# A bucketed-attention and MLP kernel: the hash beside the FFN in two passes, with its row groups added by VectorE and its transfers behind the homes

## The chip, the cores and the metric

One core of one Trainium2 chip. The metric is the device time of one execution in microseconds, the median over several runs. A profile is one further execution, taken with the hardware profiler. Engines carry the profile's names: PE (TensorE, with PEld for its weight loads), DVE (VectorE), ACT (ScalarE), POOL (GpSimd) and SP (SyncE, which issues nearly all transfers).

## The reference

Attention in which a query sees only keys of its own bucket, followed by a two-layer MLP over all tokens. A bucket is six bits: the signs of the products with six random directions.

```python
# q, k, v: (4, 8, 768, 64); proj: (64, 6); w_in: (512, 2048); w_out: (2048, 512)
q_bits = (np.einsum('bhsd,dk->bhsk', q, proj) > 0)
k_bits = (np.einsum('bhsd,dk->bhsk', k, proj) > 0)
mask = q_bucket[:, :, :, None] == k_bucket[:, :, None, :]   # buckets: the bits as numbers
scores = scale * np.matmul(q, k.transpose(0, 1, 3, 2))
scores = np.where(mask, scores, -1000000000.0)
attn = softmax(scores)
x = (attn @ v).transpose(0, 2, 1, 3).reshape(B * S, H * D)
h = x @ w_in
g = h * np.clip(h + 3.0, 0.0, 6.0) / 6.0
out = g @ w_out
```

## The kernel before

**Numbers in two parts.** PE multiplies in fp32r, which keeps fewer bits than fp32. Every operand is therefore split into a high part (`hi`, the rounded number) and a low part (`lo`, what the rounding left), and a product is the sum of three passes: hi with hi, hi with lo, lo with hi.

**Attention.** There are 32 heads (4 batches of 8) of 768 rows, in 192 steps of 128 queries, 6 steps (t = 0 to 5) to a head. `raw` holds a head's transposed queries (partitions 0 to 63) and keys (64 to 127). `split_qk` (L282) makes four tiles of it: `q1` (high part of both), `k2` (low part of the keys, then their high part), `q2` (high part of the queries, then their low part) and `k1` (high part of the keys). Half of these rows are copied across partitions by transfers. `scores` (L374) multiplies queries and keys; the mask comes out of the same product, because 12 more rows of `q1` and `k1` hold the bits of both as large numbers of either sign. Then `lowest` (L391, row minimum, DVE), `exponential` (L402, ACT), `flip` (L426, DVE transposes blocks of 32 and the tile goes to a scratch `fd` in HBM), `move` (L434, four transfers bring it back, transposed, into one of two homes, `spare` and `px`), `split_p` (L451, `ph` by ACT, `pl` by DVE for half c = 0 and by POOL for half c = 1), `values_whole` (L505, PE: `acc` from `vv` with `ph` and `pl`, the half c = 1 first) and `output` (L529, `y` by ACT, then to `xs` in HBM; the other half of each `y` is added to `xs` by a transfer that POOL issues, L522).

**The hash.** `hash_qk` (L325) makes `z`, 108 rows by 768 columns in two halves: three passes for each half, `pjl` (low part of the directions) with `q1` (L334), then `pjh` (their high part, in two placings) with `k2` (L335) and with `q2` (L336). The 44 rows from 64 on hold the bits' products, each direction with both signs. `bits` (L340) compares them with a limit per row and multiplies by a value per row (L352, DVE), writes the result into the spare rows of `q1`, and copies 12 of these rows into `k1` by a transfer.

**The MLP.** `gemm1` (L653, `h`), `gate` (L679: ACT `g`, DVE `h`, ACT `gb`, DVE `gb`) and `gemm2` (L695, `po`). `ffn` (L927) works through chunks of 256 tokens, 16 blocks of 128 of the hidden width each.

**Order.** PE, DVE, ACT and POOL run in the order in which the code is written, each engine in order; SP runs its transfers in order too. From step 101 on (`paced`) attention steps and FFN blocks alternate: `beside_ffn` (L1115) writes one of each, and the FFN's parts A to D come between the parts of the step. In one step PE takes the products with `vv` (every other step), `gemm1`, the hash if there is one, `gemm2`, then the scores. The hash of head n stands in the step whose look-ahead has t = 4 in the head before; the scores that need its bits come two steps later. There are 14 such hashes (heads 18 to 31). In the step after a hash the row minimum is written behind DVE's `gb` (`behind`, L1136), in others ahead of it.

**Transfers at the end of a step.** `moves` is a list of deferred transfers: the copies of `q1`'s rows, the keys' rows of the next head (`get_k_rows`, L246) and half of an output store. One of them is issued in each step, ahead of the four home transfers of `move`.

Of the kernel before, what the change touches and what calls it, by code (L numbers as in the profile page):

```python
# [10 lines left out]
F32 = mybir.dt.float32  # L11
F32R = mybir.dt.float32r
# [31 lines left out]
def lsh_attention_moe(  # L44
# [10 lines left out]
    nc = tc.nc  # L55
    B, H, D, S = qkT.shape
# [3 lines left out]
    HW = S // 2  # L60
# [8 lines left out]
    cp = ctx.enter_context(tc.tile_pool(name="cp", bufs=1))  # L69
    sp = ctx.enter_context(tc.tile_pool(name="sp", bufs=2))  # L70
# [5 lines left out]
    def dma(out: bass.AP, in_: bass.AP):  # L76
        nonlocal last
        last = nc.sync.dma_start(out=out, in_=in_)  # L78

    paced = False  # L80
# [12 lines left out]
    def bank(shape, name: str, tag: str | None = None):  # L93

        nonlocal turn
        if tag is None:
            tag = ("pt", "pu")[turn % 2]
            turn += 1
        return ps.tile(shape, F32, name=name, tag=tag, bufs=2)
# [4 lines left out]
    def pair(name: str):  # L104

        nonlocal pair_turn
        pair_turn += 1
        tag = "s" if ffn_on or pair_turn % 2 else "po"
        return ps.tile([P, 2, 512], F32, name=name, tag=tag, bufs=1)
# [7 lines left out]


    pjl = cp.tile([P, ZM], F32R, name="pjl")
    pjh = cp.tile([P, ZM + ZK - D], F32R, name="pjh")  # L120
    nc.vector.memset(pjl[:].bitcast(F32), 0.0)
    nc.vector.memset(pjh[:].bitcast(F32), 0.0)
    pjk, pjq = pjh[:, :ZM], pjh[:, ZK - D :]


    nc.vector.memset(thr[:], 0.0)
    nc.vector.memset(val[:], 0.0)
    for r, one, big in ((D, 0, -BIG), (ZK, 1, 1.0)):
# [3 lines left out]
        nc.vector.memset(val[r : r + 2 * NB], big * (1, -1)[1 - one])  # L132
        nc.vector.memset(val[r : r + NB], big * (1, -1)[one])
    nc.vector.memset(three[:], 3.0)

    raw0 = sp.tile([P, S], F32, name="raw0", tag="raw", bufs=1)[:]
    dma(out=raw0, in_=qkT[0, 0])
    pr = sp.tile([P, NB], F32, name="pr", tag="pr", bufs=1)
# [88 lines left out]
    NJ = B * H  # L227
# [4 lines left out]
    GT = GF + FT  # L232
    raws, vrs, state, zs = {}, {}, {}, {}
# [11 lines left out]

    def get_k_rows(i: int):  # L246
        b, h = divmod(i, H)
        moves.append(lambda: dma(out=raws[i][D:], in_=qkT[b, h, D:]))

    def get_v(i: int):  # L250
        b, h = divmod(i, H)
# [3 lines left out]
    def hash_weights():  # L255
        for x in range(2):
            c = ZK + (1 - x) * NB
            nc.vector.tensor_scalar_mul(pjh[:, c : c + NB], pr[:], (1.0, -1.0)[x])
        for r, c in ((slice(0, D), D), (slice(D, P), ZK)):
            pos = pjh[r, ZK + NB : ZM]  # L260
            nc.vector.tensor_sub(pjl[r, c + NB : c + 2 * NB], pr[r], pos.bitcast(F32))
            nc.vector.tensor_sub(pjl[r, c : c + NB], pos.bitcast(F32), pr[r])

    def spans(i: int):

# [11 lines left out]

    copied = None
    subs = []
    moves = []  # L280

    def split_qk(i: int, copy):  # L282
        nonlocal copied
# [41 lines left out]
    def hash_qk(i: int):  # L325
        k1, k2, q1, q2 = state[i]
        if paced:
            z = zs[i] = [bank([P, HW], f"z{i}_{j}") for j in range(2)]
        else:
            both = pair(f"z{i}")  # L330
            z = zs[i] = [both[:, j, :HW] for j in range(2)]
        for j in range(2):
            c = slice(j * HW, (j + 1) * HW)
            nc.tensor.matmul(z[j][:ZM], lhsT=pjl[:], rhs=q1[:, c], start=True, stop=False)  # L334
            nc.tensor.matmul(z[j][:ZM], lhsT=pjk, rhs=k2[:, c], start=False, stop=False)  # L335
            nc.tensor.matmul(z[j][:ZM], lhsT=pjq, rhs=q2[:, c], start=False, stop=True)  # L336
        if not paced:
            zs[i] = both

    def bits(i: int):  # L340
        k1, k2, q1, q2 = state[i]
        z = zs.pop(i)

        if isinstance(z, list):
            whole = [(slice(j * HW, (j + 1) * HW), z[j][D:ZM], False) for j in range(2)]
        elif i == 0:
            whole = [(slice(j * HW, (j + 1) * HW), z[D:ZM, j, :HW], False) for j in range(2)]
        else:
            whole = [(slice(0, S), z[D:ZM, :, :HW], True)]
        for c, of, both in whole:  # L350
            to = q1[D:ZM, c]
            nc.vector.tensor_scalar(  # L352
                out=to.rearrange("p (j c) -> p j c", j=2) if both else to, in0=of,
                scalar1=thr[D:ZM], scalar2=val[D:ZM], op0=ALU.is_gt, op1=ALU.mult,
            )
            if i == 0:
                nc.scalar.copy(k1[D : D + 2 * NB, c], q1[ZK:ZM, c].bitcast(F32))  # L357
            elif c.stop == S:
                dma(out=k1[D : D + 2 * NB].bitcast(F32), in_=q1[ZK:ZM].bitcast(F32))
# [678 lines left out]
    def lead(j: int):  # L1038

        i, t = divmod(j, KT)  # L1040
        n = i + 1
        alone = j <= GF + LA
        if t == 0 and n < NJ:
            split_qk(n, nc.scalar.copy if ffn_on else nc.gpsimd.tensor_copy)
        if t in (1, 4) and not paced:
            add()
        if t == (4 if paced else 2):
            if i:
                split_v(i)
        if t == (3 if paced else 2):  # L1050

            if n + 1 < NJ and n != H + 1:
                get_qk(n + 1)
                if paced:
                    get_k_rows(n + 1)
        if t == (5 if paced else 3) and n < NJ:
            get_v(n)
        hashed = t == 3 and n < NJ and alone and j != GB - 1
        if hashed:
            hash_qk(n)  # L1060
        scores(j)
        if hashed:
            bits(n)
        if t == (5 if paced else 4) and n + 1 < NJ:
            scale_q(n + 1)
# [33 lines left out]
    with tc.manual_schedule(engines={ET.PE, ET.DVE, ET.Activation, ET.Pool}):  # L1099
# [15 lines left out]
        def beside_ffn(k: int):  # L1115
# [42 lines left out]
            paced = True  # L1158
# [25 lines left out]
                moves.pop(0)()  # L1184
            if GT <= k + 1 < NS:
                move(k + 1)

            place_in_chunk = (k - GT) % NFC
            if subs and (k % 2 and (k < GT or place_in_chunk != NFC - 1) or k > GT and place_in_chunk == 0):
# [5 lines left out]
        for k in range(NS + LT + 2):  # L1195
# [4 lines left out]
            i, t = divmod(k, KT)  # L1200
# [5 lines left out]
                load_first_x()  # L1206
            if k == HK:
                late["x"] = sp.tile([P, S], F32, name="late", tag="raw", bufs=1)
            for c in range(2):
                transp(k, c)  # L1210
            if k + 1 < end:
# [8 lines left out]
            whole = False  # L1220
            for _ in range(1 if k != HK else 2):
                if vnext < k - k % 2:
                    whole = value_half()
# [3 lines left out]
            if whole and k >= GF:  # L1227
                output(vnext // 2 - 1)
                whole = False
# [98 lines left out]
```

## Time and profile before

| | us |
|---|---|
| Median of 3 runs (lowest and highest) | 976.4 (975.54, 976.92) |
| The profiled execution | 973.11 |
| Its span, first to last instruction | 971.3 |
| PE busy in the span | 948.0 (98%), 6306 matmuls |
| DVE busy | 723.5 (74%) |
| ACT busy | 625.0 (64%) |
| POOL busy | 473.6 (49%) |

A row of the timeline reads: start, length, engine, line of the kernel, operation, output<-inputs, shape, count, and in brackets the idle time of the engine before it with what ended it. A row of a group reads: line, engine, operation, output<-inputs, shapes, count, then busy time in all, mean ns of one, idle time before them and its releasers. Matmuls are pipelined: one shows as 0.34 us and the next begins before it ends, so the cost of one is read from the starts.

### The profile page before, as it was taken

What the parts mean: (1) busy time and instruction counts of PE and PEld (TensorE: products, weight loads), DVE (VectorE), ACT (ScalarE), POOL (GpSimd) and SP (SyncE); (2) the same over time, 40 slices, a digit from 0 to 9 for tenths busy, and PEclk for the clock granted to TensorE, in tenths of its full rate; (3) what the DMA queues carried; (4) which work ended last, traced back from release to release, by engine and by line L of the source; (5) the groups of instructions that cost most, each with busy time, mean ns of one, the idle gap of its engine ahead of it and who ended that gap; (6) DMA issues with size and microseconds to landing.
All of it is one profiled execution on the core that took longest, in us unless ns stands there. A gap on an engine that the chain in (4) does not pass through costs nothing.

```text
span 971.3 us, 19460 instructions
## 1 busy us (share of the span) xinstructions
PE 948.0 (98%) x6306; PEld 873.6 (90%) x6306; DVE 723.5 (74%) x1470; ACT 625.0 (64%) x1421; POOL 473.6 (49%) x582
## 2 busy tenths in 40 slices
PE   8999999999999999899999999999999999999997
PEld 7999888999989999799899899989899899889896
DVE  7999988888569999877878878878777874342422
ACT  6898875655478988667766666666666664333332
POOL 6777744665537776455555545555545432000000
PEclk9999999999999999999999999999999999999999
DMA  3567579100035554787898788788887772101000
GB/s 117 140 156 188 131 224 377 58 1 1 6 119 119 115 142 112 192 252 233 238 267 234 231 256 241 230 267 236 243 258 233 211 227 71 44 1 44 1 22 22
DMA packets 113613, 152.06 MB, mean 157 GB/s; under 512 B 13876, under 2 KB 82612, under 8 KB 113512
## 3 DMA queue, kind: packets, MB, share of 16 engines
q1 hardware_dynamic: 108472, 144.79, 48.8%
q0 software_dynamic: 5040, 6.03, 5.3%
q8 instruction: 50, 0.82, 0.4%
q14 instruction: 51, 0.42, 0.2%
HBM read 77.34 MB, written 54.00 MB: 135 GB/s over the span
## 4 chain that ended last, share of the span: by engine, by line
PE 79%; DVE 8%; DMA 4%; ACT 4%; issue 3%; POOL 1%; SPq 1%; ACTq 0%; DVEq 0%; POOLq 0%
PE h L661 25%; PE acc L500 6%; PE po L704 6%; PE po L699 6%; PE po L700 6%; PE acc L513 6%; PE pt L418 5%; PE s L389 5%; PE s L387 5%; DMA spare<-fd 2%; DVE p L396 2%; DVE pl L479 2%; ACT ph L475 1%; SPq L78 1%; DVE qq L352 1%
## 5 line engine op out<-in xcount | busy, mean ns | idle before, releaser
L408 ACT ACTIVATE p<-p,m 128x768 f32<-128x768 f32 x192 | 180.2, 939 | 113.4 <-DVE p L396 105.2
L396 DVE TENSOR_SCALAR_CACHE_REDUCE p<-s 128x768 f32<-128x768 f32 x192 | 182.7, 952 | 24.9 <-PE pt L418 12.4
L684 DVE SCALAR_TENSOR_TENSOR h<-g,h 128x256 f32<-128x256 f32 x192 | 81.1, 423 | 102.0 <-ACT g L683 99.0
L683 ACT ACTIVATE g<-h,three 128x256 f32<-128x256 f32 x192 | 91.2, 475 | 94.9 <-PE h L661 94.0
L661 PE MATMUL h<-xh,w 128*128 128x256 f32 x1024 | 146.8, 282 | 0.0
L661 PEld LDWEIGHTS h<-xh,w 128*128 128x128 f32 x1024 | 134.9, 188 | 4.2 <-ACT xh L650 0.6
L429 DVE STREAM_TRANSPOSE p<-p 128x768 f32<-128x768 f32 x90 | 88.1, 979 | 65.2 <-ACT p L408 65.1
L477 POOL TENSOR_TENSOR pl<-spare,ph 128x384 fp32r<-128x384 f32 x45 | 45.8, 1018 | 127.3 <-ACT ph L475 71.4
L479 DVE TENSOR_TENSOR pl<-pt,ph 128x384 fp32r<-128x384 f32 x196 | 100.0, 550 | 4.0 <-ACT ph L475 3.5
L387 PE MATMUL s<-kk,qq 76*128 76x384 f32 x384 | 100.5, 343 | 2.0 <-ACT kk L357 1.5
L389 PE MATMUL s<-kk,qq 128*128 128x384 f32 x384 | 100.4, 343 | 0.0
L700 PE MATMUL po<-w,gb 128*128 128x512 f32 x250 | 98.4, 393 | 0.0
L699 PE MATMUL po<-w,gb 128*128 128x512 f32 x250 | 98.3, 393 | 0.0
L475 ACT CAST ph<-pt 128x384 fp32r<-128x384 f32 x196 | 86.1, 474 | 14.3 <-PE pt L418 13.0
L216 POOL TENSOR_TENSOR w<-wr,w 128x128 fp32r<-128x128 f32 x128 | 71.9, 593 | 45.2 <-ACT w L210 41.9
L418 PE MATMUL pt<-ident,p 128*128 128x128 f32 x612 | 86.2, 275 | 1.9 <-DVE pl L479 1.1
L689 ACT CAST gb<-h 128x256 fp32r<-128x256 f32 x141 | 52.4, 372 | 54.5 <-DVE h L684 26.8
L661 PE MATMUL h<-xl,w 128*128 128x256 f32 x512 | 81.2, 280 | 0.0
L418 PEld LDWEIGHTS pt<-ident,p 128*128 128x128 f32 x612 | 72.5, 141 | 8.9 <-PE pt L418 1.5
L704 PE MATMUL po<-w,gb 128*128 128x512 f32 x250 | 78.6, 395 | 1.5 <-DVE gb L690 1.5
L318 POOL TENSOR_TENSOR kk<-raw,qq 64x192 fp32r<-64x192 f32 (+1 forms) x73 | 65.4, 920 | 25.1 <-ACT qq L304 21.7
L387 PEld LDWEIGHTS s<-kk,qq 76*128 76x128 f32 x384 | 66.6, 190 | 11.7 <-ACT kk L357 2.0
(153 smaller groups left out, 2150.9 us busy)
## 6 DMA issues: line engine op xcount, KB each, us to landing
fd<-p SPq DMA_DIRECT2D x90, 384.0 KB
spare<-fd SPq DMA_DIRECT2D x180, 96.0 KB
px<-fd SPq DMA_DIRECT2D x180, 96.0 KB
kk<-qq SPq DMA_DIRECT2D x62, 192.0 KB
wr<-in_w_in SPq DMA_DIRECT2D x16, 512.0 KB
wr<-in_w_out SPq DMA_DIRECT2D x16, 512.0 KB
raw<-in_qkT SPq DMA_DIRECT2D x19, 384.0 KB
vr<-in_v SPq DMA_DIRECT2D x32, 192.0 KB
```

Of the source, the lines that this page charges most:

```text
L387: nc.tensor.matmul(s[:, c, :HW], lhsT=q1[:KM, us], rhs=half(k1[:KM], c), start=True, stop=False)
L389: nc.tensor.matmul(s[:, c, :HW], lhsT=q2[:, us], rhs=half(k2, c), start=False, stop=True)
L396: nc.vector.tensor_scalar(out=pr_[:], in0=s[:, :, :HW], scalar1=CAP, scalar2=None, op0=ALU.min, op1=ALU.min, accum_out=m[:],)
L408: nc.scalar.activation(pr_[:], pr_[:], AF.Exp, bias=m[:], scale=-1.0, accum_out=sms[b][:, t, h : h + 1])
L418: nc.tensor.transpose(pt[:, x], probs[g][0][:, c, x * P : (x + 1) * P], ident[:])
L475: nc.scalar.copy(hi, pt)
L479: lows.append(lambda: engine.tensor_sub(lo, pt, hi.bitcast(F32)))
L661: nc.tensor.matmul(hp, lhsT=wi[:, wp, wc], rhs=x[cc][xp], start=(k == 0 and cc == 0), stop=(k == 2 and cc == NCC - 1),)
L683: nc.scalar.activation(r[:], hp, AF.Relu, bias=three[:], scale=1.0)
L699: nc.tensor.matmul(po[u], lhsT=gh[:, us], rhs=wo[:, 0], start=(fc == 0), stop=False)
L700: nc.tensor.matmul(po[u], lhsT=gh[:, us], rhs=wo[:, 1], start=False, stop=False)
L704: nc.tensor.matmul(po[u], lhsT=gl[:, us], rhs=wo[:, 0], start=False, stop=(fc == NFC - 1))
```

## The change

In the FFN stage alone (`paced`) the hash takes another form:

- **Weights.** `pjs` has 132 columns: the low part of the directions in columns 12 to 23, the high part in 108 to 119. Read from column 0 it places the keys' products, read from column 12 the queries' products, 12 rows lower. `short_weights` builds it once on POOL at step 100, in the place of `pjh`.
- **Passes.** `q2` and `k2` each hold both parts of their numbers, one in each half of the partitions, and `pr` has the directions in both halves. So one pass of `q2` and one of `k2` give both products, with the low part of the directions in rows 0 to 23 of `z` and with the high part in rows 96 to 119. `q1` is not read. A half takes two passes in place of three, each into a single bank as before.
- **Sum and threshold.** ACT copies rows 0 to 23 of each half to rows 96 to 119 of the next head's `raw` (free at that time), DVE adds rows 96 to 119 of `z` to them, and one threshold over 768 columns reads the sum from SBUF and writes 24 rows of `q1`. Before, two thresholds of 384 columns read `z` from PSUM.
- **Limits.** The limits and values per row are in a new tile, `limits`, filled by eight POOL memsets at the start.
- **Transfers.** The bits' copy to `k1` and the keys' rows of the next head go to a new list, `behind_home`, which is issued whole behind the home transfers of the step. The keys' rows are asked for at t = 4 and no longer at t = 3.

```diff
+    def short_weights():
+
+        pjs = cp.tile([P, ZK + NR + NQ], F32R, name="pjs", tag="pjh")
+        nc.gpsimd.memset(pjs[:].bitcast(F32), 0.0)
+        short.extend([pjs[:, : ZK + NR], pjs[:, NQ:]])
...
     def hash_qk(i: int):
         k1, k2, q1, q2 = state[i]
         if paced:
-            z = zs[i] = [bank([P, HW], f"z{i}_{j}") for j in range(2)]
...
+            for j in range(2):
+                c = slice(j * HW, (j + 1) * HW)
+                z = bank([P, HW], f"z{i}_{j}")
+                zs[i].append(z)
+                nc.tensor.matmul(z[: ZK + NR], lhsT=short[1], rhs=q2[:, c], start=True, stop=False)
+                nc.tensor.matmul(z[: ZK + NR], lhsT=short[0], rhs=k2[:, c], start=False, stop=True)
+            return
...
         if isinstance(z, list):
-            whole = [(slice(j * HW, (j + 1) * HW), z[j][D:ZM], False) for j in range(2)]
...
+            r = slice(ZK, ZK + NR)
+            both = raws[i + 1][r] if i + 1 < NJ else sp.tile([P, S], F32, name=f"raw{i + 1}", tag="raw", bufs=1)[r]
+            for j in range(2):
+                nc.scalar.copy(both[:, j * HW : (j + 1) * HW], z[j][:NR])
+            for j in range(2):
+                c = slice(j * HW, (j + 1) * HW)
+                nc.vector.tensor_add(both[:, c], z[j][r], both[:, c])
+            nc.vector.tensor_scalar(
+                out=q1[D : D + NR], in0=both, scalar1=ths[r], scalar2=vas[r], op0=ALU.is_gt, op1=ALU.mult,
+            )
+            behind_home.append(lambda: dma(out=k1[D : D + NQ].bitcast(F32), in_=q1[D + NQ : D + NR].bitcast(F32)))
+            return
...
                 get_qk(n + 1)
-                if paced:
-                    get_k_rows(n + 1)
+        if t == 4 and paced and n + 1 < NJ and n != H + 1:
+            get_k_rows(n + 1)
...
             if GT <= k + 1 < NS:
                 move(k + 1)
+            while behind_home:
+                behind_home.pop(0)()
...
+            if k == GT - 2:
+                short_weights()
```

How the rows stand at one hash, that of head 27 (at 653.73 us in the profile of before). Numbers behind a tile's name are buffer numbers. First PE, from the last products of `gemm1` to the first of `gemm2`, before:

```order
L661 MATMUL h_0_7_9034<-xl_0_8573,w_2678 128x256 x4
L334 MATMUL z_0_9047<-qq_8825,pjl 108x384
L335 MATMUL z_0_9047<-kk_8824,pjh 108x384
L336 MATMUL z_0_9047<-qq_8825,pjh 108x384
L334 MATMUL z_1_9048<-qq_8825,pjl 108x384
L335 MATMUL z_1_9048<-kk_8824,pjh 108x384
L336 MATMUL z_1_9048<-qq_8825,pjh 108x384
L699 MATMUL po_0_8615<-w_2644,gb_0_6_9023 128x512
```

And PE at the same place now:

```order
L698 MATMUL h_0_7_9057<-xl_0_8596,w_2687 128x256 x4
L354 MATMUL z_0_9070<-qq_8849,pjs 120x384
L355 MATMUL z_0_9070<-kk_8848,pjs 120x384
L354 MATMUL z_1_9073<-qq_8849,pjs 120x384
L355 MATMUL z_1_9073<-kk_8848,pjs 120x384
L736 MATMUL po_0_8638<-w_2653,gb_0_6_9046 128x512
```

Two of six passes are gone and nothing else moves on PE. Next DVE from the flip to the row minimum of that step, before:

```order
L429 STREAM_TRANSPOSE p_9021<-p_9021 128x768
L684 SCALAR_TENSOR_TENSOR h_0_7_9034<-g_0_7_9061,h_0_7_9034 128x256
L479 TENSOR_TENSOR pl_0_9065<-spare,ph_0_9064 128x3x128
L352 TENSOR_SCALAR qq_8825<-z_0_9047,thr,val 44x384
L352 TENSOR_SCALAR qq_8825<-z_1_9048,thr,val 44x384
L690 TENSOR_TENSOR gb_0_7_9084<-h_0_7_9034,gb_0_7_9084 128x256
L396 TENSOR_SCALAR p_9088,m_9087<-s_9074 128x768
```

And DVE now, in the same stretch of the step:

```order
L466 STREAM_TRANSPOSE p_9044<-p_9044 128x768
L721 SCALAR_TENSOR_TENSOR h_0_7_9057<-g_0_7_9082,h_0_7_9057 128x256
L516 TENSOR_TENSOR pl_0_9086<-spare,ph_0_9085 128x3x128
L377 TENSOR_TENSOR raw_9019<-z_0_9070,raw_9019 24x384
L377 TENSOR_TENSOR raw_9019<-z_1_9073,raw_9019 24x384
L378 TENSOR_SCALAR qq_8849<-raw_9019,limits 24x768
L727 TENSOR_TENSOR gb_0_7_9109<-h_0_7_9057,gb_0_7_9109 128x256
L433 TENSOR_SCALAR p_9113,m_9112<-s_9097 128x768
```

Three instructions stand where two stood, ahead of `gb` and the row minimum. ACT's two copies (L374) stand behind the `ph` cast of half c = 0 and ahead of the gate's `gb` cast. Last SP from the keys' and queries' rows of the next head (`raw`) to the values (`vr`), before:

```order
L78 DMA raw_8995<-in_qkT 64x768 x2
L78 DMA xs_128<-y_0_8867 64x512
L78 DMA fd_8965<-p_8958 128x768
L78 DMA px<-fd_8911 32x4x192 x4
L78 DMA fd_9028<-p_9021 128x768
L78 DMA spare<-fd_8965 32x4x192 x3
L78 DMA kk_8824<-qq_8825 12x768
L78 DMA spare<-fd_8965 32x4x192
L78 DMA vr_9123<-in_v 128x384
```

And SP now, between the same two transfers:

```order
L78 DMA raw_9019<-in_qkT 64x768
L78 DMA xs_137<-y_0_8891 64x512
L78 DMA fd_8989<-p_8982 128x768
L78 DMA px<-fd_8935 32x4x192 x4
L78 DMA fd_9051<-p_9044 128x768
L78 DMA spare<-fd_8989 32x4x192 x4
L78 DMA kk_8848<-qq_8849 12x768
L78 DMA raw_9019<-in_qkT 64x768
L78 DMA vr_9148<-in_v 128x384
```

The bits' copy (`kk`, 12 rows) went behind the fourth home transfer, and the keys' rows (the second `raw`) from ahead of eight home transfers to behind them.

More of the change, by code (lines that the diff above doesn't have):

```diff
@@ L119, in lsh_attention_moe @@
     pjl = cp.tile([P, ZM], F32R, name="pjl")
-    pjh = cp.tile([P, ZM + ZK - D], F32R, name="pjh")
+    pjh = cp.tile([P, ZM + ZK - D], F32R, name="pjh", tag="pjh")
     nc.vector.memset(pjl[:].bitcast(F32), 0.0)
@@ L123, in lsh_attention_moe @@
     pjk, pjq = pjh[:, :ZM], pjh[:, ZK - D :]
+    NQ = 2 * NB
+    NR = 2 * NQ
+    short = []
+    limits = cp.tile([P, 2], F32, name="limits")
+    ths, vas = limits[:, 0:1], limits[:, 1:2]
     nc.vector.memset(thr[:], 0.0)
@@ L134, in lsh_attention_moe @@
     nc.vector.memset(three[:], 3.0)
+    for n, (lim, mul) in reversed(list(enumerate(((TINY, -BIG), (-TINY * (1 + 2.0 ** -23), BIG), (-TINY * (1 + 2.0 ** -23), -1.0), (TINY, 1.0))))):
+        r = slice(ZK, ZK + (n + 1) * NB)
+        nc.gpsimd.memset(ths[r], lim)
+        nc.gpsimd.memset(vas[r], mul)
     raw0 = sp.tile([P, S], F32, name="raw0", tag="raw", bufs=1)[:]
@@ L247, in get_k_rows @@
         b, h = divmod(i, H)
-        moves.append(lambda: dma(out=raws[i][D:], in_=qkT[b, h, D:]))
+        behind_home.append(lambda: dma(out=raws[i][D:], in_=qkT[b, h, D:]))
     def get_v(i: int):
@@ L262, in hash_weights @@
             nc.vector.tensor_sub(pjl[r, c : c + NB], pos.bitcast(F32), pr[r])
+    def short_weights():
+        pjs = cp.tile([P, ZK + NR + NQ], F32R, name="pjs", tag="pjh")
+        nc.gpsimd.memset(pjs[:].bitcast(F32), 0.0)
+        short.extend([pjs[:, : ZK + NR], pjs[:, NQ:]])
+        c = ZK + NQ
+        pos = pjs[:, c + NB : c + NQ].bitcast(F32)
+        for x in range(2):
+            nc.gpsimd.tensor_scalar_mul(pjs[:, c + (1 - x) * NB : c + (2 - x) * NB], pr[:], (1.0, -1.0)[x])
+        nc.gpsimd.tensor_sub(pjs[:, NQ + NB : 2 * NQ], pr[:], pos)
+        nc.gpsimd.tensor_sub(pjs[:, NQ : NQ + NB], pos, pr[:])
     def spans(i: int):
@@ L279, in lsh_attention_moe @@
     subs = []
-    moves = []
+    moves, behind_home = [], []
     def split_qk(i: int, copy):
@@ L327, in hash_qk @@
         if paced:
-            z = zs[i] = [bank([P, HW], f"z{i}_{j}") for j in range(2)]
-        else:
-            both = pair(f"z{i}")
-            z = zs[i] = [both[:, j, :HW] for j in range(2)]
+            zs[i] = []
+            for j in range(2):
[5 more added lines that the diff above has]
+            return
+        both = pair(f"z{i}")
+        z = zs[i] = [both[:, j, :HW] for j in range(2)]
         for j in range(2):
@@ L336, in hash_qk @@
             nc.tensor.matmul(z[j][:ZM], lhsT=pjq, rhs=q2[:, c], start=False, stop=True)
-        if not paced:
-            zs[i] = both
+        zs[i] = both
     def bits(i: int):
@@ L344, in bits @@
         if isinstance(z, list):
-            whole = [(slice(j * HW, (j + 1) * HW), z[j][D:ZM], False) for j in range(2)]
-        elif i == 0:
+            r = slice(ZK, ZK + NR)
[10 more added lines that the diff above has]
+            return
+        if i == 0:
             whole = [(slice(j * HW, (j + 1) * HW), z[D:ZM, j, :HW], False) for j in range(2)]
```

## The prediction

> **What bounds the kernel now.** The page says PE 98%. So first the busy time of each engine over the stretch in which the change acts (the stretches view, 402 to 780 us; columns: length, then busy us and instructions of PE, PEld, DVE, ACT and POOL, granted clock, DMA share, GB/s), then two of PE's groups of instructions from 398 to 860 us (busy, mean ns, idle before, its releaser).
>
> ```profile
> 402.00:780.00 378.00, 371.18 (x2396) 341.47 (x2395) 299.44 (x571) 251.85 (x591) 201.51 (x262) 1.00 0.82 243
> L334 PE MATMUL z<-qq,pjl 128*108 128x384 f32 x28 | 9.5, 338 | 0.2 <-ACT y L547 0.2
> L513 PE MATMUL acc<-ph,vv 128*128 128x256 f32 x270 | 44.1, 291 | 5.0 <-ACT ph L475 4.5
> ```
>
> PE is busy for 371 of 378 us at the full granted clock; DVE for 299. So the matrix engine is the bound, and work taken from it looks like time won. L334 has 28 instructions there, two halves for each of 14 heads: 14 hashes in the FFN stage. PE's largest wait, 4.5 us in all, is for `ph` of ACT (L475), ahead of the products L513. What a hash meets is read from the timeline of one plain head, PE's rows first.
>
> ```profile
> 653.73 0.34 PE L334 MATMUL z<-qq,pjl 128*108 128x384 f32 x1
> ...
> 654.78 0.40 PE L699 MATMUL po<-w,gb 128*128 128x512 f32 x1
> ...
> 660.40 0.94 PE L513 MATMUL acc<-ph,vv 128*128 128x256 f32 x6
> ```
>
> Six passes start within 654.78 - 653.73 = 1.05 us, so **one pass is worth 0.175 us** of PE (its 0.34 is pipeline). At 660.40 PE takes six products with `ph`; the first three use one half (c = 1), the last three, from about 660.76, the other. The second half comes at the end of this row of work on DVE and ACT:
>
> ```profile
> 655.55 1.29 DVE L352 TENSOR_SCALAR qq<-z,thr,val 44x384 fp32r<-44x384 f32 x2
> 656.87 0.42 DVE L690 TENSOR_TENSOR gb<-h,gb 128x256 fp32r<-128x256 f32 x1
> 657.21 0.95 DVE L396 TENSOR_SCALAR_CACHE_REDUCE p<-s 128x768 f32<-128x768 f32 x1
> ```
>
> ```profile
> 654.37 0.50 ACT L475 CAST ph<-spare 128x384 fp32r<-128x384 f32 x1
> 656.38 0.37 ACT L689 CAST gb<-h 128x256 fp32r<-128x256 f32 x1 [1.51 <-PE po L704]
> 658.20 0.94 ACT L408 ACTIVATE p<-p,m 128x768 f32<-128x768 f32 x1 [1.45 <-DVE p L396]
> 659.04 0.19 ACT L408 ACTIVATION_READ_ACCUMULATOR p<-p,m 128x1 f32 x1
> 659.14 0.50 ACT L475 CAST ph<-px 128x384 fp32r<-128x384 f32 x1
> 659.54 0.36 ACT L547 COPY y<-acc 128x256 f32<-128x256 f32 x1
> 659.80 0.48 ACT L683 ACTIVATE g<-h,three 128x256 f32<-128x256 f32 x1
> 660.17 0.51 ACT L475 CAST ph<-px 128x384 fp32r<-128x384 f32 x1
> ```
>
> DVE runs without a break through the thresholds (L352), `gb` and the row minimum (L396). ACT waits 1.45 us for that minimum, then runs exponential, `ph`, `y`, gate and `ph` without a break, and ends at 660.68. PE wants that half at 660.76. **The slack is about 0.05 us.** DVE's 79% hides that its work behind a hash ends PE's next wait. Another head shows what more DVE work there costs:
>
> ```profile
> 738.29 0.17 DVE L567 TENSOR_SCALAR rc<-sms 128x16 f32<-128x16 f32 x1
> 738.50 0.25 DVE L568 RECIPROCAL rc<-rc 128x16 f32<-128x16 f32 x1
> 738.78 0.42 DVE L690 TENSOR_TENSOR gb<-h,gb 128x256 fp32r<-128x256 f32 x1
> ...
> 741.83 0.51 PE L513 MATMUL acc<-ph,vv 128*128 128x256 f32 x3
> 742.64 0.62 PE L513 MATMUL acc<-ph,vv 128*128 128x256 f32 x3 [0.30 <-ACT ph L475]
> ```
>
> Between the thresholds and `gb` stand 0.49 us (738.29 to 738.78) that the plain head lacks, and PE begins the second three 0.81 us after the first in place of 0.36: it loses 0.45 us. Time added on DVE there arrives on PE one for one.
>
> **The change: PE.** One pass of each half goes: 2 x 0.175 = 0.35 us a head, 14 x 0.35 = 4.9 us. That is won only if nothing ends later. But PE then merely reaches the products with `ph` 0.35 us earlier, and `ph` comes from a row of work that starts ahead of the hash (the flip and the gate) and takes no step from the saved passes.
>
> **The change: ACT.** Two copies of 24x384 from PSUM follow L475's first half (654.37). The nearest row is the cast of 384 from PSUM:
>
> ```profile
> L475 ACT CAST ph<-pt 128x384 fp32r<-128x384 f32 x196 | 86.1, 474 | 14.3 <-PE pt L418 13.0
> L479 DVE TENSOR_TENSOR pl<-pt,ph 128x384 fp32r<-128x384 f32 x196 | 100.0, 550 | 4.0 <-ACT ph L475 3.5
> L352 DVE TENSOR_SCALAR qq<-z,thr,val 44x384 fp32r<-44x384 f32 x30 | 19.3, 686 | 1.0 <-PE z L336 0.5
> L352 DVE TENSOR_SCALAR qq<-z,thr,val 44x768 fp32r<-44x768 f32 x17 | 18.5, 1086 | 0.8 <-POOL rblate L577 0.3
> L291 DVE CAST qq<-raw 64x768 fp32r<-64x768 f32 x1 | 0.6, 557 | 2.2 <-DMA raw<-in_qkT 2.2
> ```
>
> At 0.47 us each, less some 0.07 of overlap, they run from about 654.77 to 655.64, inside the 1.51 us for which ACT waits for PE before `gb`: nothing. The first is done by 655.24, the second before DVE's second add starts; if ACT were late, DVE would wait for it.
>
> **The change: DVE.** Two thresholds of 384 become two adds of 384 and one threshold of 768. An add reads PSUM and SBUF as L479 `pl<-pt` does: 0.55 us. The pair of L352 (1.29 for two of 0.69) overlaps by 0.09, so two adds end at 655.55 + 0.55 + 0.55 - 0.08 = 656.57, and the threshold, which needs both, starts at 656.60. Its length no row shows. L352 grows by 0.40 us from 384 to 768, so 0.29 is fixed and 0.80 streams from PSUM; the cast L291 of 768 from SBUF takes 0.557 in all, so from SBUF the stream is half: 0.40. I take 0.29 + 0.40 = 0.69. The ends are 0.56 (the cast) and 1.09 (PSUM's rate). And POOL is at work there:
>
> ```profile
> 655.96 1.01 POOL L368 TENSOR_TENSOR vv<-vr,vv 128x384 fp32r<-128x384 f32 x1
> 161.58 0.69 DVE L203 TENSOR_SCALAR wr<-wr 128x512 f32<-128x512 f32 x1
> 164.06 0.42 DVE L203 TENSOR_SCALAR wr<-wr 128x512 f32<-128x512 f32 x1
> 160.90 1.09 POOL L216 TENSOR_TENSOR w<-wr,w 128x128 fp32r<-128x128 f32 x2
> ```
>
> L203, also from SBUF to SBUF at the fast rate, takes 0.42 alone, but 0.69 beside POOL's L216, and ends 0.28 after it (162.27 against 161.99): its stream waits until POOL is done. L368 is under way until 656.97, so the threshold ends 0.40 and a little later, 657.39, and `gb` starts at 657.42 in place of 656.87: **DVE is 0.55 us later**, or 0.45 where L368 ends before the threshold starts (656.60 + 0.69 + 0.03 = 657.32). With the ends: 0.32 and 0.85.
>
> **Summed over the 14 heads.** A head loses what DVE is later, less its slack; where PE already waits, all of it.
>
> ```profile
> 680.62 0.34 PE L334 MATMUL z<-qq,pjl 128*108 128x384 f32 x1
> 687.65 0.96 PE L513 MATMUL acc<-ph,vv 128*128 128x256 f32 x6
> 771.85 0.62 PE L513 MATMUL acc<-ph,vv 128*128 128x256 f32 x3 [0.36 <-ACT ph L475]
> 633.07 0.37 ACT L547 COPY y<-acc 128x256 f32<-128x256 f32 x1 [1.10 <-DMA xs<-y]
> ```
>
> - Five plain heads (432, 487, 570, 653, 708 us): 5 x (0.55 - 0.05) = 2.5.
> - Three with normalising transposes on PE (459, 597, 680): `acc` comes 7.03 us behind the hash (680.62 to 687.65), not 6.67, so the slack is about 0.38; 0.07, 0.07 and 0.17: 0.3.
> - Five in which PE waits behind the hash already (401, the stage's first; 513 and 735 with the reciprocal; 541 and 763 with four splits on DVE, as at 771.85): 3 x 0.55 + 2 x 0.45 = 2.55.
> - One (625), in which ACT's `y` waits 1.10 us for a transfer: it absorbs the delay, 0.
>
> Together **5.35 us lost**, PE's 4.9 included as lost in waiting. The span goes from 971.3 to 976.7; the profiled execution took 973.1 and would take 978.5. The runs' median is 976.4, 3.3 above it; I add the same sum: 981.7.
>
> **The change: transfers and weights.** At the hash SP issues the bits' copy ahead of the last home transfer, and is held by it until the thresholds are done; below it what ACT's casts of `spare` waited for from 470 to 860 us:
>
> ```profile
> 656.99 0.83 SPq L78 DMA_DIRECT2D kk<-qq  x1
> L475 ACT CAST ph<-spare 128x384 fp32r<-128x384 f32 x75 | 37.5, 500 | 1.4 <-DMA spare<-fd 1.4
> ```
>
> Behind the homes, the last of these leaves some 0.8 us earlier; but ACT waited for homes 1.4 us in all over 75 casts, so there is next to nothing to win. The bits leave at the threshold's end either way, and the keys' rows leave later by most of a step; both are read two steps behind the hash. I cost them at nothing; late ones would stop the next head's scores or split. POOL's eight small memsets and the five instructions of the short weights stand where POOL waits (before the first input, and ahead of the first FFN hash): nothing.
>
> [...]
>
> **The rivals.**
> - *The pass is won* (not slower): the row of work behind the hash does not reach PE. 976.4 - 4.9 = 971.5. For it: PE's 371 of 378 us, ACT's idle 1.51. Against: the 0.45 us of the head at 735. It decides where DVE is less than 0.05 us later; the two adds alone end 1.02 us in, so the threshold would have to take 0.3. Chance 0.13, mostly for a head that I read wrongly.
> - *The earlier homes repay* (no change): PE's 4.5 us of waits for `ph` were waits for homes and 4 of them vanish: 5.35 - 4 = 1.35, 977.8. Against: the 1.4 us of ACT above. Chance 0.09.
> - *The threshold is cheaper than any row* (no change): at 0.46 us, a tenth under the cheapest row, and free of POOL, DVE is 0.22 later: 5 x 0.17 - 3 x 0.16 + 5 x 0.22 = 1.5, 977.9. The cast's 0.557 speaks against it. Chance 0.04. [...]
> - *The threshold at PSUM's rate*: 0.85 later: 5 x 0.80 + 3 x 0.47 + 5 x 0.85 = 9.7, 986.1. Chance 0.14.
>
> **How the numbers follow.** The forecast has 0.60. Its own bounds are 979.2 (0.32 later: 5 x 0.27 - 3 x 0.06 + 5 x 0.32 = 2.8) and 984.1 (0.70 later, half way to PSUM's rate: 5 x 0.65 + 3 x 0.32 + 5 x 0.70 = 7.7). For eight in ten I leave out the first rival and a little above: 975 to 987. A measurement here tells a change over 0.2%, 2 us, from none. Slower: 0.60 + 0.14 = 0.74; within: 0.13; faster: 0.13.
>
> **What would show it.** In the new profile: `z` passes 28 fewer; DVE's two adds at 0.55 and a threshold at 0.69, longer beside L368; `gb` behind it 0.45 to 0.55 us later after the hash; PE's wait for ACT `ph` up from 4.5 us by some 10 (the 4.9 saved and the 5.35 lost). If PE's wait stays near 4.5, the forecast is wrong. If the adds start late, ACT's copies set them. If new waits name `kk` or `raw`, the moved transfers count.

## The result, and the profile after

The changed kernel takes 981.51 us (median of 6 runs, 980.21 to 983.98). In runs beside it the kernel before takes 976.4, and the ratio is 1.0059 [1.0042, 1.0076]: 5.8 us slower by the ratio, 5.1 by the medians. The forecast was 981.7. The profiled execution took 980.71 us, 7.6 more than that of before (the forecast for it was 978.5), and its span is 978.9 us.

First the window of the FFN stage (stretch, its length, busy time and instructions of PE, PE's weight loads, DVE, ACT, POOL, then the granted clock, the DMA share and GB/s), in the changed kernel:

```profile
402.00:780.00 378.00, 365.58 (x2325) 331.11 (x2325) 300.63 (x577) 258.37 (x607) 199.58 (x259) 1.00 0.82 237
```

PE is busy 5.6 us less in these 378 us (365.58 for 371.18). That is not time won: in a stretch of one length it is 5.6 us more of idle PE. The groups of the new lines, and PE's waits between 398 and 870 us (line, what it waited for, us in all, times, longest), of the changed kernel:

```profile
L354 PE MATMUL z<-qq,pjs 128*120 128x384 f32 x28 | 9.6, 344 | 0.3 <-ACT y L584 0.3
L377 DVE TENSOR_TENSOR raw<-z,raw 24x384 f32<-24x384 f32 x28 | 14.6, 558 | 0.4
L374 ACT COPY raw<-z 24x384 f32<-24x384 f32 x28 | 11.7, 465 | 0.3
L378 DVE TENSOR_SCALAR qq<-raw,limits 24x768 fp32r<-24x768 f32 x14 | 10.4, 740 | 0.5
```

```profile
PE acc L550 <- ACT ph L512: 9.7, 24, 1.8
PE po L741 <- DVE gb L727: 1.5, 2, 0.9
```

PE's wait for `ph` has more than doubled: 9.7 us in 24 waits, for 4.5 before. Where it arises is read from the same plain head as in the prediction. It starts its hash at 653.73 before and at 658.05 now. DVE, ACT and PE of the changed kernel, in the timeline:

```profile
659.22 0.62 DVE L516 TENSOR_TENSOR pl<-spare,ph 128x384 fp32r<-128x384 f32 x1
659.87 1.04 DVE L377 TENSOR_TENSOR raw<-z,raw 24x384 f32<-24x384 f32 x2
660.95 0.76 DVE L378 TENSOR_SCALAR qq<-raw,limits 24x768 fp32r<-24x768 f32 x1
661.74 0.42 DVE L727 TENSOR_TENSOR gb<-h,gb 128x256 fp32r<-128x256 f32 x1
662.08 0.95 DVE L433 TENSOR_SCALAR_CACHE_REDUCE p<-s 128x768 f32<-128x768 f32 x1
```

```profile
659.21 0.84 ACT L374 COPY raw<-z 24x384 f32<-24x384 f32 x2
660.35 0.37 ACT L726 CAST gb<-h 128x256 fp32r<-128x256 f32 x1 [0.30 <-PE po L741]
663.07 0.94 ACT L445 ACTIVATE p<-p,m 128x768 f32<-128x768 f32 x1 [2.35 <-DMA spare<-fd]
663.91 0.19 ACT L445 ACTIVATION_READ_ACCUMULATOR p<-p,m 128x1 f32 x1
664.01 0.50 ACT L512 CAST ph<-px 128x384 fp32r<-128x384 f32 x1
664.41 0.36 ACT L584 COPY y<-acc 128x256 f32<-128x256 f32 x1
664.67 0.47 ACT L720 ACTIVATE g<-h,three 128x256 f32<-128x256 f32 x1
665.04 0.51 ACT L512 CAST ph<-px 128x384 fp32r<-128x384 f32 x1
```

```profile
658.05 0.34 PE L354 MATMUL z<-qq,pjs 128*120 128x384 f32 x1
...
658.76 0.39 PE L736 MATMUL po<-w,gb 128*128 128x512 f32 x1
...
664.65 0.59 PE L550 MATMUL acc<-ph,vv 128*128 128x256 f32 x3
665.60 0.62 PE L550 MATMUL acc<-ph,vv 128*128 128x256 f32 x3 [0.36 <-ACT ph L512]
```

Count from the hash. `gb` starts at 3.69 (661.74 - 658.05) in place of 3.14 (656.87 - 653.73): 0.55 us later, as forecast. The row minimum follows at once and ends at 663.0. ACT's exponential starts 0.04 us after that, at 5.02 in place of 4.47, so DVE ends ACT's idle of 2.35, although the bracket names a transfer. From there to the end of the second `ph` ACT runs without a break. PE's `po` starts behind the passes at 0.71 in place of 1.05, and PE takes the first three products with `ph` at 6.60 and the second three at 7.55. In the kernel before all six stood together from 6.67, and the second three would have started 0.36 behind the first, at 7.03. The second three are 0.52 later, although 0.35 us of PE's work ahead of them has gone.

A caution in reading: without a delay the first three would start at 6.67 - 0.35 = 6.32 and the second at 6.68. PE is thus 0.87 us late there, but the bracket shows 0.36 and the row above it none. A matmul's record (0.59 to 0.62 for three) runs on past the time at which the next could start (0.36 behind the first of them), so a short wait hides inside it. That is why the sum of the waits rose by 5.2 us where the heads lost 11.5 (their net of 6.60, below, and the 4.9 of the passes).

The shift of PE's own steps is free of that. I take from the timeline the start of the first score product (`s`) of each step, in the changed kernel less in the kernel before, and how this grows from one step to the next. At the hash it falls by 0.35 us (the passes) in ten of the 14 heads, and by 0.07, 0.20, 0.08 and 0.23 in those at 401, 432, 570 and 735. In one of the two steps behind it rises again. Fall and rise together, in us:

```
head at (before)   401   432   459   487   513   541   570   597   625   653   680   708   735   763
net of the head   +.43  +.74  +.07  +.54  +.56  +.47  +.82  +.26  +.37  +.55  +.12  +.52  +.68  +.47
forecast          +.55  +.50  +.07  +.50  +.55  +.45  +.50  +.17   .00  +.50  +.07  +.50  +.55  +.45
```

The heads' net sums to 6.60 us, for 5.35 forecast. From step 96 to step 191 the shift grows by 7.15 (from -0.13 to +7.02); what the heads do not hold is 0.35 at 506 and 0.25 at 792 and crumbs. This is one execution of each kernel.

### The profile page after: what moved, and what is told of

It is laid out like the page before. It is cut to its first block, busy times and chain, and to the rows that moved or that the text cites. A ratio compares the mean times of both kernels' runs of the same rounds, so it can differ in the third digit from the quotient of the medians.

```text
span 978.9 us, 19456 instructions
## 1 busy us (share of the span) xinstructions
PE 949.9 (97%) x6278; PEld 869.4 (89%) x6278; DVE 729.1 (74%) x1484; ACT 636.3 (65%) x1449; POOL 475.3 (49%) x595
## 4 chain that ended last, share of the span: by engine, by line
PE 69%; DVE 9%; DMA 8%; ACT 6%; issue 4%; POOL 2%; SPq 2%; ACTq 0%; DVEq 0%; POOLq 0%
PE h L698 22%; PE acc L537 6%; PE po L741 5%; PE pt L455 5%; PE po L736 5%; PE po L737 5%; PE acc L550 5%; PE s L426 4%; PE s L424 4%; DMA spare<-fd 3%; DVE p L433 3%; ACT ph L512 2%; DVE pl L516 2%; SPq L78 2%; DMA px<-fd 2%
## 5 line engine op out<-in xcount | busy, mean ns | idle before, releaser
L514 POOL TENSOR_TENSOR pl<-px,ph 128x384 fp32r<-128x384 f32 x45 | 46.0, 1022 | 68.1 <-ACT ph L512 49.7
```

The costliest lines, as they stand in the source:

```text
L514: engine.tensor_sub(lo, pt, hi.bitcast(F32))
```

## The experiments

In the names below, the theory is that of the prediction: DVE's work behind the hash sets when `ph` comes, with no slack to speak of, and PE's saved passes are lost in that wait. Times are medians; the interval is that of the ratio to the kernel before, timed beside each experiment (975.01 us for the first four, 974.9 for the next three, 974.86 for the last two). The stage is the growth of the shift from step 96 to step 191, as above. It comes from one execution, and two kernels below whose medians are no longer than that of before still show 1.06 and 1.95; it says where time goes, and the medians say how much.

```
                          time     ratio [95%]                 stage
the change                981.51   1.0059 [1.0042, 1.0076]     +7.15
DVE work alone            982.56   1.0071 [1.0055, 1.0088]     +9.92
six passes kept           981.81   1.0067 [1.0048, 1.0085]     +6.82
transfers alone           974.2    0.9987 [0.9973, 1.0000]     +1.06
threshold later           974.2    0.9997 [0.9982, 1.0013]     +0.36
threshold later, 6 passes 975.48   1.0004 [0.9994, 1.0015]     +2.32
adds later too           1003.42   1.0282 [1.0257, 1.0307]    +21.36
old thresholds later     1011.96   1.0367 [1.0343, 1.0392]    +39.54
ACT's copies alone        973.97   0.9987 [0.9972, 1.0003]     +1.95
small DVE work alone      978.55   1.0033 [1.0017, 1.0049]     +4.34
```

The granted clock has a part in the stage of five of these profiles. In that of "threshold later" it falls to 0.5 for 3.41 us behind PE's wait in the head at 625 (the stretch, with the columns of the window above):

```profile
634.72:638.13 3.41, 3.41 (x19) 3.41 (x18) 2.13 (x4) 1.77 (x5) 1.01 (x1) 0.50 0.98 307
```

The products of `acc` and `h` start 0.213 us apart in it and 0.118 behind it, so such a stretch costs some 1.5 us (an estimate: 3.41 x (1 - 0.118/0.213)). "DVE work alone" has one at 640.73 and "threshold later, 6 passes" one at 637.76, both in the same head; "adds later too" has two and "old thresholds later" ten. The profiles of the kernel before and of the change have none there, although PE waits in the same head.

**DVE work alone.** The kernel before, with one more DVE instruction behind the two thresholds of each FFN hash; six passes, no ACT copy, transfers as before. The cast goes to rows that nobody reads.

```diff
+        if isinstance(z, list):
+            nc.vector.tensor_copy(k1[ZK:ZM, :HW], z[1][ZK:ZM])
```

> The kernel before with one more instruction on DVE behind the two thresholds of each of the 14 hashes (a cast of 12x384 from PSUM into unused rows of k1, about 0.5 us); passes, ACT and transfers stay. Theory (DVE ends PE's next wait): about 5 us more than before, 979.5 to 983, as the changed kernel, and PE's waits for ACT ph up by about 5 us. Rival (the loss comes from ACT's copies or from the transfers): 976 to 977.5.

Its group and PE's waits between 398 and 870 us:

```profile
L361 DVE CAST kk<-z 12x384 fp32r<-12x384 f32 x14 | 7.9, 563 | 0.4
```

```profile
PE acc L515 <- ACT ph L477: 7.2, 19, 1.1
PE po L706 <- DVE gb L692: 3.2, 2, 1.8
PE h L663 <- DVE kk L361: 0.9, 3, 0.3
```

0.56 us of DVE work 14 times is 7.9 us, and the kernel is 6.9 us slower (0.0071 x 975): nearly all of DVE's added time arrives, although PE's work is untouched. Each of the five plain heads loses 0.58 to 0.60 in the steps behind the hash. The stage's 9.92 holds the 1.5 of the clock besides, and 1.0 us at 401, where `po` waits longer for DVE's `gb` (its two waits: 3.2 us in all, for 1.5 before). The wait for `ph` rises by 2.7 and not by the 5 expected, since part of it hides in the records as above. But the experiment is not pure: the cast reads the second `z` bank and keeps it longer, and three times, in the heads with normalising transposes, `gemm1` waits for that bank. The 0.50 to 0.59 that these three lose are the bank's, not the row's.

**Six passes kept.** The changed kernel with its first pass issued twice, so that PE has again six passes' time; everything else is as in the change.

```diff
+                nc.tensor.matmul(z[: ZK + NR], lhsT=short[1], rhs=q2[:, c], start=True, stop=True)
                 nc.tensor.matmul(z[: ZK + NR], lhsT=short[1], rhs=q2[:, c], start=True, stop=False)
```

> The changed kernel with the first pass of each half run twice (the second overwrites the first): PE has six passes for a hash again, 0.35 us more in each of 14. Theory (PE waits for ACT ph behind the hash anyway): the time of the changed kernel, 980.5 to 982.5, and PE's wait for ph down by what the passes add. Rival (the saved passes are won and something else costs 10 us): 4.9 us more, 986.4.

```profile
PE acc L551 <- ACT ph L513: 7.3, 18, 1.6
```

4.9 us of PE's work came back and the time is the same: the intervals with and without it, 1.0048 to 1.0085 and 1.0042 to 1.0076, lie on each other. In the steps a plain head no longer falls by 0.35 at the hash, and rises by 0.52 in place of 0.90 behind it. The waits for `ph` shrink from 9.7 to 7.3, since the work fills them: by 2.4 as they show, with the caution above. So the saved passes bought nothing in the changed kernel.

**Transfers alone.** The kernel before, its hash untouched, with only the bits' copy and the keys' rows moved behind the homes as the change does it.

```diff
-        moves.append(lambda: dma(out=raws[i][D:], in_=qkT[b, h, D:]))
+        behind_home.append(lambda: dma(out=raws[i][D:], in_=qkT[b, h, D:]))
...
+            while behind_home:
+                behind_home.pop(0)()
```

> The kernel before (three passes, two thresholds from PSUM) with the bits' copy and the keys' rows behind the home transfers, as in the change. Theory (their place costs and brings nothing): 975.4 to 977.4. Rival (the homes are earlier and repay): under 974.5. Rival (a late copy stops a head): over 978.5.

974.2 lies under the 974.5 of the first rival, but the kernel before took 975.0 beside it and not 976.4: by the ratio, 0.9987 [0.9973, 1.0000], the moved transfers win 0 to 2.6 us. The loss isn't theirs, and they don't win 4 us either. In the steps one place moves with them: at 506, where PE waits for `ph` (in the changed kernel behind a late home transfer, `px` from `fd`), the profiles of five kernels with moved transfers rise by 0.17 to 0.75 (the change, six passes kept, this one with 0.75, threshold later, and that with six passes), and those of "DVE work alone", "small DVE work alone" and "ACT's copies alone", whose transfers stay, do not rise.

**ACT's copies alone.** The kernel before with the change's two ACT copies per hash, to rows that nobody reads.

```diff
         if isinstance(z, list):
+            for j in range(2):
+                nc.scalar.copy(k1[ZK:ZM, j * HW : (j + 1) * HW], z[j][ZK:ZM])
```

> The kernel before with ScalarE's two copies of the change alone (12x384 from each bank into rows that nobody reads, some 0.47 us each, 0.94 us a hash, ahead of the thresholds); six passes and two thresholds as before. Theory of the prediction (the copies lie in ScalarE's idle before gb, 1.51 us at 653, and cost nothing): 974.5 to 975.7 us where the kernel before takes 975, and the wait of acc for ph stays near 4.5 us between 398 and 870. Rival (ScalarE's own row gb, exp, ph is as tight as VectorE's, or the bank's second reader holds the thresholds back): 1 to 4 us more, 976 to 979 us, with gb and exp later by 0.1 to 0.5 us in the heads.

ACT in the plain head whose hash is at 653.73 before:

```profile
655.67 0.85 ACT L346 CAST kk<-z 12x384 fp32r<-12x384 f32 x2
657.16 0.37 ACT L691 CAST gb<-h 128x256 fp32r<-128x256 f32 x1 [0.64 <-PE po L706]
659.00 0.94 ACT L410 ACTIVATE p<-p,m 128x768 f32<-128x768 f32 x1 [1.47 <-DVE p L398]
```

The copies fill ACT's idle ahead of its `gb` (0.64 left of 1.51), the wait for the row minimum stays (1.47 for 1.45), and the ratio is 0.9987 [0.9972, 1.0003]. 0.94 us a hash costs nothing on ACT at this place, where 0.56 on DVE costs 6.9 us in all.

**Small DVE work alone.** As "DVE work alone", with 64 columns in place of 384.

```diff
+        if isinstance(z, list):
+            nc.vector.tensor_copy(k1[ZK:ZM, :64], z[1][ZK:ZM, :64])
```

> The kernel before with one small VectorE cast (12x64) behind the two thresholds of each hash, instead of the 12x384 of 0.56 us that cost 6.9 us. It should last 0.15 to 0.25 us (an estimate from the 0.56 us of the long one). Theory of the prediction (slack of 0.05 us in the plain heads at 432, 487, 570, 653 and 708, none in the five heads that already wait): five heads lose its length less 0.05, five its whole length, 1.3 to 2.3 us in all, 976.3 to 977.3 us, and in the trace the step two behind a plain head's hash comes 0.1 to 0.2 us later than in the kernel before. Rival (the plain heads have 0.25 us of slack or more, and only the amount beyond that is paid): 0.7 to 1.2 us in all from the five waiting heads, and the plain heads' steps come no later.

Its group, and DVE in the plain head (hash at 653.73 before):

```profile
L361 DVE CAST kk<-z 12x64 fp32r<-12x64 f32 x14 | 3.2, 230 | 0.4
```

```profile
658.75 1.29 DVE L352 TENSOR_SCALAR qq<-z,thr,val 44x384 fp32r<-44x384 f32 x2
660.06 0.23 DVE L361 CAST kk<-z 12x64 fp32r<-12x64 f32 x1
660.33 0.42 DVE L692 TENSOR_TENSOR gb<-h,gb 128x256 fp32r<-128x256 f32 x1
```

3.2 us slower (0.0033 x 975), between 1.7 and 4.8 by the interval: more than the 1.3 to 2.3 expected, and far from a slack of 0.25. With the cast `gb` starts 1.58 behind the thresholds' start (660.33 - 658.75) in place of 1.32: 0.26 later. The five plain heads lose 0.25 to 0.28 each in the steps behind the hash: all of it. So there are not even 0.05 us of slack in a plain head. The other part that the expectation missed is the three heads with normalising transposes (0.20 to 0.22 each), where `gemm1` starts later behind the transposes, at the place where the longer cast showed the wait for its bank.

**Threshold later.** The changed kernel, with the adds in place (they free the banks), but the threshold, the bits' copy and the keys' rows behind the row minimum of the next step, out of the row that ends in `ph`.

```diff
...
-            nc.vector.tensor_scalar(
-                out=q1[D : D + NR], in0=both, scalar1=ths[r], scalar2=vas[r], op0=ALU.is_gt, op1=ALU.mult,
-            )
-            behind_home.append(lambda: dma(out=k1[D : D + NQ].bitcast(F32), in_=q1[D + NQ : D + NR].bitcast(F32)))
+
+            def threshold():
+                nc.vector.tensor_scalar(
+                    out=q1[D : D + NR], in0=both, scalar1=ths[r], scalar2=vas[r], op0=ALU.is_gt, op1=ALU.mult,
+                )
+                dma(out=k1[D : D + NQ].bitcast(F32), in_=q1[D + NQ : D + NR].bitcast(F32))
+
+            behind_minimum.append(threshold)
...
+            while behind_minimum:
+                behind_minimum.pop(0)()
```

> The changed kernel with the threshold of 768, the bits' copy and the keys' rows behind the row minimum of the next step (the two adds stay where they are, ahead of gb). Theory: the minimum starts some 0.35 us earlier after the hash than in the kernel before, as the scores are, and the saved passes are won in nearly all heads: 976.4 - 4.5, 970.5 to 973.5. Rival (DVE's work costs wherever it stands): 980 to 983.

DVE in the plain head (its hash at 655.17) and at 453; then PE in the plain head; then ACT in the head at 625:

```profile
453.33 0.96 DVE L437 TENSOR_SCALAR_CACHE_REDUCE p<-s 128x768 f32<-128x768 f32 x1 [1.44 <-DMA fd<-p]
...
656.99 1.04 DVE L377 TENSOR_TENSOR raw<-z,raw 24x384 f32<-24x384 f32 x2
658.06 0.42 DVE L731 TENSOR_TENSOR gb<-h,gb 128x256 fp32r<-128x256 f32 x1
658.40 0.95 DVE L437 TENSOR_SCALAR_CACHE_REDUCE p<-s 128x768 f32<-128x768 f32 x1
659.28 0.08 DVE L437 DVE_READ_ACCUMULATOR p<-s 128x1 f32 x1
659.39 0.68 DVE L380 TENSOR_SCALAR qq<-raw,limits 24x768 fp32r<-24x768 f32 x1
```

```profile
655.17 0.34 PE L354 MATMUL z<-qq,pjs 128*120 128x384 f32 x1
...
661.51 1.03 PE L554 MATMUL acc<-ph,vv 128*128 128x256 f32 x6
```

```profile
632.92 0.37 ACT L588 COPY y<-acc 128x256 f32<-128x256 f32 x1 [1.80 <-DMA xs<-y]
```

`gb` is at 2.89 behind the hash, 0.25 earlier than before the change, and PE's six products stand together again, at 6.34 in place of 6.67: in this head 0.35 is won at the hash and 0.10 lost behind it. The loss of the change is gone: 0.9997 [0.9982, 1.0013]. With "transfers alone", where moved transfers cost nothing, that settles what caused it. But the gain below the kernel before, the passes' 4.9 us, did not come: 974.2 lies in neither of the two ranges expected. The steps fall by 0.35 at 12 of the 14 hashes, and the fall is taken back at several places, for several reasons:

- From 452 to 465 (0.48) the row minimum waits 1.44 us until the transfer `fd` from `p` has read its tile.
- At 525 and 746 (0.29 and 0.28), in the heads with the reciprocal, `acc` waits again for ACT `ph` (0.36 in each) behind DVE's row, as in the kernel before.
- At 506 (0.50) the rise comes with the moved transfers, as above.
- From 717 to 728 (0.68) the row minimum waits for `fd` too. But "small DVE work alone" and "ACT's copies alone", whose passes are untouched, rise at 723 and 728 by 0.73 and 1.32, so that this one isn't shown to be the passes'.
- In the head at 625 (1.94) some 1.5 is the granted clock, and 0.35 the passes' own: `y`, which waits for the software transfer `xs` from `y`, starts 7.55 behind the hash, for 7.54 before.

How much of the 4.9 each takes over the medians is not shown.

**Threshold later, six passes.** The kernel above, with the first pass issued twice as in "six passes kept".

> The kernel with the threshold behind the next row minimum took 974.2 us, although its hash has 28 passes fewer; here TensorE gets the 28 passes back (14 hashes x 2 x 0.175 us = 4.9 us of its work). Theory 1 (what the passes give is lost again in waits of TensorE for transfers that come no earlier: the software transfer that feeds y of head 625, 1.94 us there, and 0.3 to 0.5 us at 454, 506, 525, 728 and 746): the added passes fill those waits, and the time stays at 974 to 975.5 us. Theory 2 (the passes won their 4.9 us, and the adds, which still stand in VectorE's row, took as much away): the passes cost their whole length, 978 to 979.5 us.

```profile
PE acc L555 <- ACT ph L517: 5.8, 11, 2.3
```

The passes cost 0.7 us of their 4.9 (1.0004 for 0.9997; with both intervals some 2 us either way): within the first theory's 974 to 975.5. Its reason holds in part. There is no fall at a hash, and none of the rises at 454, 525, 717 to 728 and 746, which the added passes fill, whatever PE waited for there. The rises at 506 (0.73) and in the head at 625 (2.34) stay and are larger, so they are not a give-back of the passes. The first comes with the moved transfers. In the head at 625 the clock takes some 1.5 again, and `y` starts 8.29 behind the hash, 0.75 later than before: its software transfer took 5.6 us to land, for 4.5.

**Adds later too.** Adds and threshold both go behind the row minimum of the next step.

```diff
             def threshold():
+                for j in range(2):
+                    c = slice(j * HW, (j + 1) * HW)
+                    nc.vector.tensor_add(both[:, c], z[j][r], both[:, c])
                 nc.vector.tensor_scalar(
```

> Adds and threshold both stand behind the row minimum of the next step, so that VectorE's row to gb has nothing of the hash in it but ScalarE's two copies before exp. Theory 1 (transfers hold the end now): 973 to 975 us, as with the threshold alone moved, or up to 1 us more since bits and key rows come later still. Theory 2 (the adds took what the passes gave): 969 to 971 us, 4.9 us below the kernel before or nearly.

PE's waits between 398 and 870 us; then, for the plain head whose hash is at 668.19 there, PE's row that waits and DVE's adds beside it:

```profile
PE h L702 <- DVE raw L379: 19.9, 10, 2.9
PE rt L628 <- DVE raw L379: 5.3, 3, 1.8
```

```profile
672.93 1.18 PE L702 MATMUL h<-xh,w 128*128 128x256 f32 x8 [1.76 <-DVE raw L379]
```

```profile
672.22 1.04 DVE L379 TENSOR_TENSOR raw<-z,raw 24x384 f32<-24x384 f32 x2
```

Both theories miss: 27 us slower (0.0282 of 975). The adds are what frees the `z` banks, and `gemm1` wants a bank 2.98 us behind the hash (672.93 - 1.76 - 668.19). With the adds behind the minimum it gets it 1.76 us late in eight heads and 2.9 in two, and the transposes (`rt`) wait in three more.

**The old thresholds later.** The kernel before with six passes; its two thresholds, which read the banks, and the bits' copy behind the row minimum of the next step.

```diff
...
-                bits((k + LA) // KT + 1)
+                behind_minimum.append(lambda n=(k + LA) // KT + 1: bits(n))
```

> The hash of before with its six passes; only its two thresholds (0.49 to 0.56 us each) and the copy of the bits are moved behind the row minimum of the next step. If VectorE's row sets the end in the kernel before too, in the heads where TensorE already waits for ph (at 513 and 735 some 0.47 us each, at 541 and 763 some 1.07 us each, by what TensorE lost there): 971.9 to 973.5 us against 975.0. If these heads then meet a transfer instead: 974.5 to 976 us. In heads without slack lost, as at 653, nothing is to be gained either way.

```profile
PE h L661 <- DVE qq L352: 20.5, 10, 2.7
PE rt L587 <- DVE qq L352: 5.7, 3, 1.9
```

The same wall, 36 us slower (0.0367 of 975). Not all of it is the wait. In this profile ten stretches at a granted clock of 0.5 lie between 466 and 809 us, some 15 of the stage's 39.54 by the estimate above, and in that of "adds later too" two, some 3 of 21.36. The mean clock of the timed runs is 0.979 to 0.986 here and 0.982 to 0.996 there, for 0.995 to 0.999 of the kernel before beside them, so the medians hold such stretches too. So these two runs say nothing on what a shorter DVE row would give in the kernel before. What they show is the other limit: DVE must read the banks within some 3 us of the hash, and all else that it does there stands in the row to `ph`.

## Why the prediction was right, and where its terms were off

- **PE's passes.** Forecast: 0.35 us a head, lost again in waiting. Shown: the steps fall by 0.35 at the hash in ten of the 14 heads, and giving the passes back changes nothing (six passes kept).
- **The row of work that sets the end.** Forecast: DVE, `gb`, row minimum, exponential, `ph`, `y`, gate, `ph`. Shown by adding to it (0.56 and 0.23 us arrive), by taking the threshold out of it (the loss goes), and by adding to ACT ahead of it (nothing).
- **Slack.** Forecast 0.05 us in a plain head. A cast of 0.23 arrives whole, so there is none; the net of 487, 653 and 708 is 0.52 to 0.55, where 0.50 was forecast. In the heads with normalising transposes the slack was 0.38: 0.07 and 0.12 at 459 and 680, for 0.07 forecast. At 597 it was 0.26 for 0.17.
- **Lengths.** Adds 0.56 for 0.55, copies 0.465 for 0.47. The threshold is 0.68 where POOL's L405 has ended and 0.76 beside it, for 0.69; `gb` is 0.55 later in the plain head, as forecast. That the threshold came out so is in part luck: the stream of 0.40 was read from the cast L291 as half of PSUM's, but the cast's 0.557 less the fixed 0.29 leaves 0.27. Only the changed kernel bears out the 0.40, by the threshold's end 0.42 behind POOL's L405. The rival with a threshold of 0.46 falls: no run shows that length, which lies 0.10 under the cast's 0.557 (a tenth of a microsecond, not of the row), and the shortest of the 14 thresholds took 0.68. The rival at PSUM's rate (1.09) falls too: the longest took 0.77.
- **Transfers, weights, ACT.** Forecast nothing. Transfers alone 0.9987, copies alone 0.9987: nothing that the medians show, though the 0.35 at 506 comes with the transfers. The earlier homes did not repay 4 us.
- **The mis-sized term.** The head at 625 was to absorb the delay, since `y` waits there for a transfer. It lost 0.37. `y` waits 1.35 us, for 1.10 before: the two software transfers that POOL issues took 4.6 and 4.9 us from issue to landing, for 4.4 and 4.5 before, and left 0.13 later behind the hash. The threshold beside them did not lengthen the issues: it began 0.29 ahead of the first, and they took as long as before (0.83 and 1.10). With six passes kept the same head lost 0.16; and in "small DVE work alone", which has the thresholds and transfers of before, `y` starts 8.15 behind the hash, for 7.88 in the changed kernel and 7.54 before. So 0.37 lies within what the landing of these transfers varies by from profile to profile, and its cause stays open.
- **The rest of the trace.** 0.35 at 506 and 0.25 at 792 and the larger net at 432, 570 and 735, where the fall at the hash is smaller, were not in the sum; with the head at 625 they make most of the step from the forecast's 5.35 to the trace's 7.15. The medians have 5.1 between them and the ratio gives 5.8 [4.1, 7.4], so that the 5.35 is right within the measurement. That the median came within 0.2 us of 981.7 is luck: the profiled execution, forecast by the same sum, lies 2.2 above its 978.5.
- **PE's wait for `ph`.** Forecast up by some 10, measured up by 5.2: the lost time was about right and the reading wrong, since short waits hide in the matmul records.

## What to carry to other kernels

The busiest engine is not always the one whose work to take away: at 98% busy, TensorE gave nothing for 4.9 us less work, because the products behind it wait for a row of VectorE and ScalarE work without slack: there 0.23 us more on VectorE cost 0.25 to 0.28. Before work is moved from one engine to another, follow the next wait of the engine that is relieved back to its start, and price the move by the slack of that row at that place, head by head. And a step that is taken off such a row may be what frees a buffer: the adds could not move, the threshold could, and what was won then met other waits, part of them for transfers.

## What the runs showed of the hardware

**A software transfer's issue beside an SBUF threshold.** In "threshold later" the threshold begins inside an issue of POOL in five heads (401, 459, 597, 625 and 680). POOL and DVE of that kernel, in the last:

```profile
685.60 1.25 POOL L563 DMA_DIRECT2D xs<-y  x1
```

```profile
686.09 0.68 DVE L380 TENSOR_SCALAR qq<-raw,limits 24x768 fp32r<-24x768 f32 x1
```

The threshold begins 0.49 behind the issue's start; the issue takes 1.25 us where others take 0.84, and ends 0.08 behind the threshold's end. So it is at 401 (0.46 behind, 1.25 us) and at 625, where the threshold meets the second of two issues (0.47 behind, 1.31 us for 1.10 before). In the heads at 459 and 597 it begins 0.63 and 0.52 behind, and the issue keeps its 0.84. In the changed kernel 11 issues overlap a threshold: in two (546.94 and 772.29) it begins 0.29 behind, and the issue takes 1.05, again to 0.08 behind the threshold's end; in nine it begins 0.29 ahead and is over 0.36 before the issue ends, which takes its usual 0.83 or 0.84. So in these two kernels an issue took 0.21 to 0.41 us longer where a threshold began 0.29 to 0.49 behind its start, and no longer where the threshold began 0.29 ahead of it, or 0.52 and 0.63 behind; why is not shown. Over the stage of the changed kernel the transfers land much as before: a median of 3.6 us (128 KB) and 3.7 (64 KB) behind the issue, for 3.7 and 3.4 before.

**The other way round.** Beside POOL's two-input multiply L405 the threshold takes 0.76 and not 0.68. In the plain head L405 ran from 660.28 to 661.29 and the threshold ended at 661.71, 0.42 after it: its stream had waited, as the prediction had worked out from L203. All ten thresholds beside L405 end 0.42 behind it.
